# Sparse attention over gathered key blocks, with mixing in full tiles, in a fused attention and mixer kernel

## The chip, the cores and the metric

The kernel runs on one core of one Trainium2 chip. The metric is the device time of one execution in microseconds (us); the figure given is the median of several executions. A profile is one further execution, recorded instruction by instruction.

## The reference

The first half is block-sparse attention (the "BigBird" pattern) over 4 batches, 8 heads, 768 positions and 64 elements a head. Positions form 24 blocks of 32. A block of queries sees its own block and the two neighbours, the first and the last block, and three sampled blocks; the first and the last query block see everything. Which blocks are sampled is an input, `sampled_blocks` of 24 x 3 integers, known only when the kernel runs.

```python
scores = scale * np.matmul(q, k.transpose(0, 1, 3, 2))
mask = np.abs(blk_i - blk_j) <= window
mask = mask | (blk_i == 0) | (blk_j == 0) | (blk_i == n_blocks - 1) | (blk_j == n_blocks - 1)
for qb in range(n_blocks):
    for kb in sampled_blocks[qb]:
        mask[qb * block:(qb + 1) * block, kb * block:(kb + 1) * block] = True
scores = np.where(mask, scores, -1000000000.0)
...
return np.matmul(attn, v).astype(np.float32)
```

The second half mixes. With x the attention's output as (batch, 768, 512), and weights of 768x256, 256x768, 512x1536 and 1536x512:

```python
xt = x.transpose(0, 2, 1)
h = np.maximum(xt @ w_tok1, 0.0) @ w_tok2
u = x + h.transpose(0, 2, 1)
h2 = np.maximum(u @ w_ch1, 0.0) @ w_ch2
return (u + h2).astype(np.float32)
```

A batch's token mixing (`w_tok`) needs all 768 rows of x of that batch; its channel mixing (`w_ch`) needs u of the rows that it treats.

## The kernel before

**Attention.** A step is a pair of heads p (four to a batch, 16 in all), a third t of the queries (256) and a third jj of the keys (256). `scores` (matmul L917) fills two banks of PSUM with keys on the partitions and queries along the row; ScalarE takes the exponential of 128x1024 elements (L930). All 768 keys are computed for every query, and the mask is put in afterwards or beforehand: in batch 0 by 24 more rows in the contraction (88 instead of 64), from batch 1 on by `cut` (L948), a product on VectorE of the exponentials with a mask of zeros and ones that GpSimd has spread over 128x6x768 elements (L731). Then comes the product with V, which carries a column of ones, so that column 65 of the result is the sum of the weights: in batch 0 `pv_stream` (L1086, full tiles of 128 rows), later `pv_halves` through the helper `halves`. VectorE divides by the sum (L1040 and L1041, in batch 0 L1099 and L1100) and writes x.

**Transposes of Q and K.** TensorE does them for pairs 0 to 7 (L823 and L858), SP's transposing DMA for pairs 8 to 15 (`crossbar`, L788).

**`halves`** (L365, matmul L375) computes everything after batch 0's attention, up to the last attention product, in pairs of matmuls on 64-row tiles: one pass over the upper and lower rows of the contraction into two banks, then a fence on SP or GpSimd (L361), then a second pass with the banks exchanged. The scores from batch 1 on are also pairs of 64-row tiles, one head each, so that TensorE keeps one shape of tile throughout. Only after the last attention product does mixing run in full 128-row tiles (`tok_full` L1296 and L1318, `ch` L1536 and L1601).

**Mixing.** `tok` and `tok_first` (batch 0, a pair at a time) do token mixing, `turn_by_crossbar` (L1145, SP) or `turn_by_pe` (L1165) and, for batch 0, `turn_first` transpose u, and `ch` does channel mixing in pieces: first layer, ReLU (ScalarE L1128 or VectorE L1130) into the tile `rc`, second layer, addition on VectorE (L1567, L1615), and a store by SP (L1572, L1626).

**What sets the order.** No engine chooses anything on the chip: a `Planner` (L104) runs at build time and writes every engine's order by hand. It keeps a clock with assumed costs, streams of TensorE work with priorities (scores, attention products, transposes, token and channel mixing), a list of operations for VectorE, ScalarE and SP with costs and due times, and the eight banks of PSUM. A table of knobs (`KN`) changes priorities along the way. `P.phase` is 0 up to the last score of batch 0, 1 while attention is left, 2 after that. Loads of Q, K and V (L447) and of weights (L455, L459, L466, L473) are issued by GpSimd.

Of the kernel before, what the change touches and what calls it, by code (L numbers as in the profile page):

```python
# [12 lines left out]
PLAN = False  # L13
BASE = dict(
    tokp=2.5, trp=2.6, toks=-0.5, back=0.5, relayk=0.8, relayv=3.0, fin=0.9, relu=2.2, cut=0.7,
# [11 lines left out]
    6: dict(fin=4.1, cps=3, trp=1.6),  # L27
    7: dict(fin=4.1, cps=3, trp=1.6),
    8: dict(fin=4.1, cps=3, trp=1.6, add=0.3, back=1.1, cut=0.5),
    9: dict(shift=6000.0),  # L30
    10: dict(fin=4.1, cps=3, trp=1.6, add=0.3, back=1.1, cut=0.5, m2=300.0, ev2=0.9, jit=300.0),
    12: dict(fin=4.1, cps=3, trp=1.6, add=0.3, back=1.1, cut=0.5, m2=300.0, ev2=0.9, jit=300.0, tokp=1.7, backp=0.9, cpo=2, m1=0.0),
    13: dict(fin=4.1, cps=3, trp=1.6, add=0.3, back=1.1, cut=0.5, m2=300.0, ev2=0.9, jit=2000.0, tokp=1.7, backp=0.9, cpo=2, m1=0.0, late=3.5, relayk=0.8),
    14: dict(m2=0.0, cch=2, m1=0.0, cut=6.0, ev4=1.2),
    16: dict(add=0.3, late=1.05, cch=2, ev4=2.0, relayk=3.5),
    17: dict(m1=0.0, back=1.1, add=0.95),
    18: dict(m1=0.0, back=1.1, add=0.95, cut=1.1, m2=300.0, cpo=2),
    19: dict(cps2=3, toks=0.4, jit=300.0, relayv=3.0, relayk=3.5),
    20: dict(m1=0.0, back=1.1, add=0.95, cut=1.1, m2=0.0, cpo=2, toks=-0.5, backp=0.45, cpm=1),
    21: dict(m1=0.0, back=1.1, add=0.95, cut=1.1, m2=0.0, cpo=2, toks=-0.5, backp=0.45, cpm=1),  # L40
    22: dict(m1=100.0, back=1.1, add=0.95, cut=6.0, m2=0.0, cpo=2, toks=-0.5, backp=0.45, cpm=1, relayk=0.8),
    23: dict(m1=100.0, back=1.1, add=0.95, cut=6.0, m2=0.0, cpo=2, toks=-0.5, backp=0.45, cpm=1, relayk=0.8, jit=300.0, cps=3),
    24: dict(m1=100.0, back=1.1, add=0.95, cut=6.0, m2=0.0, cpo=2, toks=-0.5, backp=0.45, cpm=1, relayk=0.8, jit=300.0, cps=3),
    25: dict(jit=450.0, cps2=2, relayv=4.6),
    27: dict(jit=450.0, cps2=2, relayv=4.6, cps=2, backp=0.45, cpo=2, relu=0.85),
    28: dict(jit=450.0, cps2=2, relayv=4.6, cps=2, backp=0.45, cpo=2, relu=0.85),
    29: dict(jit=450.0, cps2=2, relayv=4.6, cps=2, backp=0.45, cpo=2, relu=0.85, toks=0.4, relayk=4.5),
    30: dict(jit=450.0, cps2=2, relayv=4.6, cps=2, backp=0.45, cpo=1, relu=0.85, norm=0.6, cpm=2, backt=0.9),
    31: dict(back=1.1, cpm=1, jit=1300.0),
    32: dict(jit=450.0, cps2=2, relayv=4.6, cps=2, backp=0.45, cpo=1, relu=0.85, norm=1.0, cpm=2, backt=0.9, m1=100.0, shift=0.0),  # L50
    33: dict(tokp=0.7, cps=3, ev4=1.2, shift=-6000.0, cch=2),
    34: dict(chs=0.8, m1=100.0, ev2=1.2, cpo=2, backt=0.2),
    35: dict(jit=0.0, cpo=2, chs=1.1),
# [50 lines left out]
class Planner:  # L104
# [12 lines left out]
    def __init__(self, slots, caps):  # L117
        self.now = 0.0
        self.free_at = {"pe": 0.0, "act": 0.0, "dve": 0.0, "sp": 0.0}
# [93 lines left out]
    def step(self):  # L213
# [36 lines left out]
        for eng in ("act", "dve", "sp"):  # L250
# [9 lines left out]
            for o in self.ops:  # L260
# [4 lines left out]
                if eng == "act" and prio > 0 and self.now + cost["act"] > exp_at + KN["grace"]:  # L265
                    continue
# [28 lines left out]
def kernel(  # L295
# [10 lines left out]
    out: bass.AP,  # L306
):
    nc = tc.nc

    B, H, S, D = q.shape  # L310
    assert (B, H, S, D) == (4, 8, 768, 64)
    NC = 6
    DM, DT, DC = 512, 256, 1536
    NP = B * H // 2
    MASKVAL = -30000.0
    NV = 4
    NR = 4
    NET = KN["net"]
# [46 lines left out]
    def halves(n, cost, outs, lhs, rhs, deps, tags, begin, done, prio, ahead=0.0):  # L365
# [25 lines left out]
        for x in range(n):  # L391
            def emit(x=x):
                if x == 0:
                    begin()
# [1353 lines left out]
```

The softmax here doesn't subtract the row's maximum and nothing guards it: scores larger than these inputs give would overflow.

## Time and profile before

| what | value |
|---|---|
| device time, median of 3 runs | 244.84 us (244.62 to 245.03) |
| the profiled execution, span from first to last instruction | 243.4 us |
| mean granted TensorE clock, 1 is full | 0.999 |
| TensorE (PE) busy | 237.0 us, 97% |
| VectorE (DVE) busy | 172.1 us, 71% |
| ScalarE (ACT) busy | 170.0 us, 70% |
| GpSimd (POOL) busy | 49.5 us, 20% |
| instructions | 9647 |

The profiled execution has no device time of its own but its span, 243.4 us; the median of the runs stands 1.4 us above it. In lines of the profile L12 is line 12 of the kernel. "Busy" adds the durations of an engine's instructions where they don't overlap; "PEld" is the loading of weights into TensorE, which runs beside its matmuls; SPq, POOLq are the sequencers of SP and GpSimd, which issue DMAs, and issuing is not counted as busy. A group's line gives line, engine, operation, out<-in, count, then busy us and mean ns of one, then the engine's idle time just before these instructions and what ended most of it. The time of a matmul in such a line is that from its start to its modelled end, and matmuls overlap.

### The profile page before, as it was taken

Reading aid. Unit: us, or ns where it says so; the run is one execution under the profiler, and the core shown is the slowest. Engines: PE = TensorE matmul, PEld = TensorE weight load, DVE = VectorE, ACT = ScalarE, POOL = GpSimd, SP = SyncE. Lnnn points to the kernel's source line nnn. Section 1 sums busy time; section 2 is a strip of 40 time slices with the busy share of each in tenths; the row PEclk is TensorE's granted clock in tenths of the full one; section 3 lists DMA queues with packets and bytes.
Section 4 is the critical chain, followed back from the end, with each engine's and each line's share of the span. In section 5 each row is a group of like instructions: output and inputs, shape, how many; then the busy total and the mean of one; then the engine's idle time right before and its main releaser. Section 6 shows DMA issues by size and latency. Waiting matters only on the chain.

```text
span 243.4 us, 9647 instructions
## 1 busy us (share of the span) xinstructions
PE 237.0 (97%) x4343; PEld 170.9 (70%) x4343; DVE 172.1 (71%) x285; ACT 170.0 (70%) x187; POOL 49.5 (20%) x86
## 2 busy tenths in 40 slices
PE   7999999999999999999999999999999999999994
PEld 3689999767777677867878667677688664565444
DVE  5975987979899889799789788987687535100222
ACT  6889999868797699788778987798658400366000
POOL 8966987357710000000000000000000000000000
PEclk9999999999999999999999999999999999999999
DMA  7999999999993874131207270501030024200132
GB/s 163 166 214 203 209 207 203 206 201 196 201 180 76 132 167 137 38 118 33 40 3 89 46 155 3 154 25 67 3 67 3 5 89 127 112 3 0 43 132 86
DMA packets 39755, 26.17 MB, mean 108 GB/s; under 512 B 21985, under 2 KB 37105, under 8 KB 39713
## 3 DMA queue, kind: packets, MB, share of 16 engines
q0 software_dynamic: 15104, 12.98, 33.9%
q1 hardware_dynamic: 24064, 12.17, 20.4%
q8 instruction: 34, 0.56, 0.9%
q10 hardware_dynamic: 544, 0.39, 0.6%
q14 instruction: 9, 0.07, 0.1%
HBM read 26.74 MB, written 6.29 MB: 136 GB/s over the span
## 4 chain that ended last, share of the span: by engine, by line
PE 89%; DMA 3%; ACT 3%; POOL 2%; DVE 1%; issue 0%; POOLq 0%; DVEq 0%; ACTq 0%
PE banks L375 53%; PE banks L917 14%; PE banks L1601 9%; PE banks L1536 6%; DMA kraw<-in_k_dram 3%; ACT et L930 3%; PE banks L1086 3%; PE banks L858 1%; PE banks L1354 1%; DVE et L948 1%; POOL vraw L447 1%; PE banks L1296 1%; PE banks L1376 1%; PE banks L1318 1%; POOL ktb L517 0%
## 5 line engine op out<-in xcount | busy, mean ns | idle before, releaser
L930 ACT ACTIVATE et<-banks 128x1024 bf16<-128x1024 f32 x144 | 141.6, 1025 | 28.3 <-PE banks L917 24.5
L948 DVE TENSOR_TENSOR et<-et,mask 128x2976 bf16<-128x2976 bf16 x36 | 61.3, 1703 | 8.3 <-ACT et L930 8.2
L917 PE MATMUL banks<-qtb,ktb 64*128 64x256 bf16 (+1 forms) x576 | 63.7, 270 | 0.7 <-ACT et L930 0.2
L375 PE MATMUL banks<-uT,w_ch 64*128 64x512 bf16 (+1 forms) x576 | 60.6, 322 | 0.0
L375 PE MATMUL banks<-w_ch,rc 64*128 64x512 bf16 x384 | 54.3, 376 | 0.0
L375 PEld LDWEIGHTS <-et 64*128 64x128 bf16 x1728 | 39.2, 94 | 9.4 <-POOLq L361 3.0
L917 PEld LDWEIGHTS <-ktb 64*128 64x128 bf16 (+1 forms) x576 | 33.8, 94 | 15.1 <-issue 1.4
L375 PE MATMUL banks<-vaug,et 64*128 64x65 bf16 x1728 | 42.0, 190 | 0.2 <-issue 0.2
L375 PEld LDWEIGHTS <-w_ch 64*128 64x128 bf16 x576 | 28.6, 94 | 8.4 <-SPq L361 0.6
L1128 ACT ACTIVATE rc<-banks 128x512 bf16<-128x512 f32 (+1 forms) x28 | 21.0, 749 | 17.0 <-PE banks L1536 15.0
L1615 DVE TENSOR_TENSOR o<-banks,x 128x512 f32<-128x512 f32 x7 | 4.8, 692 | 28.2 <-PE banks L1601 28.2
L1130 DVE TENSOR_SCALAR rc<-banks 128x1024 bf16<-128x1024 f32 x17 | 20.8, 1221 | 3.4 <-PE banks L375 3.2
L375 PEld LDWEIGHTS <-rc 64*128 64x128 bf16 x384 | 17.3, 94 | 7.9 <-POOLq L361 0.5
L1601 PE MATMUL banks<-w_ch,rc 128*128 128x512 bf16 (+2 forms) x120 | 21.3, 337 | 0.0
L1601 PEld LDWEIGHTS <-rc 128*128 128x128 bf16 x120 | 10.7, 98 | 10.6 <-issue 0.8
L375 PEld LDWEIGHTS <-w_tok 64*128 64x128 bf16 x288 | 14.5, 109 | 3.3 <-POOLq L361 0.6
L1041 DVE TENSOR_TENSOR x<-banks,recip 128x256 bf16<-128x256 f32 x36 | 15.3, 425 | 1.2
L1536 PE MATMUL banks<-uT,w_ch 128*128 128x512 bf16 (+1 forms) x96 | 15.8, 326 | 0.0
L1536 PEld LDWEIGHTS <-w_ch 128*128 128x128 bf16 x96 | 9.4, 98 | 6.4
L1567 DVE TENSOR_TENSOR o<-banks,x 128x1024 f32<-128x1024 f32 x8 | 9.8, 1224 | 5.1 <-PE banks L375 5.0
L1086 PE MATMUL banks<-vaug,et 128*128 128x65 bf16 x288 | 13.1, 193 | 0.0
L1264 DVE TENSOR_TENSOR x<-banks,x 128x512 bf16<-128x512 f32 (+2 forms) x12 | 10.3, 887 | 2.9 <-PE banks L375 2.7
(122 smaller groups left out, 198.0 us busy)
## 6 DMA issues: line engine op xcount, KB each, us to landing
out_dram<-o SPq DMA_DIRECT2D x8, 512.0 KB, 3.6
w_ch<-in_moe_w_ch_dram POOLq DMA_DIRECT2D x8, 384.0 KB, 9.8
vraw<-in_v_dram POOLq DMA_DIRECT2D x10, 192.0 KB, 7.9
out_dram<-o SPq DMA_DIRECT2D x7, 256.0 KB, 2.0
kraw<-in_k_dram POOLq DMA_DIRECT2D x9, 192.0 KB, 9.2
qraw<-in_q_dram POOLq DMA_DIRECT2D x9, 192.0 KB, 8.3
w_tok<-in_moe_w_tok_dram POOLq DMA_DIRECT2D x2, 384.0 KB, 10.0
qf<-in_v_dram POOLq DMA_DIRECT2D x4, 192.0 KB, 7.8
```

What stands on the lines that cost most here:

```text
L375: mms.append(nc.tensor.matmul(out=outs()[o](x), lhsT=lhs(o, x, r), rhs=rhs(o, x, r), start=(back == 0 and x == 0), stop=(back == 1 and x = ...
L917: nc.tensor.matmul(out=ps[:, hd, 256 * i : 256 * i + 256], lhsT=ktb[n][rows, h, 256 * jj + 128 * i : 256 * jj + 128 * i + 128], rhs=qtb[n] ...
L930: nc.scalar.activation(out=ets[p, t][:, jj, :, :, :].rearrange("k i h q -> k h i q"), in_=ps.rearrange("k h (i q) -> k h i q", i=2), func= ...
L948: nc.vector.tensor_tensor(out=et, in0=et, in1=free(mask[:, 2 * lo, 256 * t + EDGE : 256 * t + EDGE + 1], 0, [[S, 2 * n], [0, 2], [1, w]]), ...
L1041: nc.vector.tensor_tensor(out=free(xs[b][:, pb // 2, 2 * t, 128 * (pb % 2) : 128 * (pb % 2) + 128], 0, [[64, 2], [256, 2], [1, 64]],), in0 ...
L1086: nc.tensor.matmul(out=po[:, hd, c, :], lhsT=et[:, jj, i, hd, 128 * c : 128 * c + 128], rhs=va[:, hd, 2 * jj + i, 0:65], start=(jj == 0 an ...
L1128: nc.scalar.activation(out=o(), in_=src(), func=AF.Relu)
L1130: nc.vector.tensor_scalar(out=o(), in0=src(), scalar1=0.0, scalar2=None, op0=ALU.max)
L1264: nc.vector.tensor_tensor(out=u, in0=src, in1=u, op=ALU.add)
L1536: nc.tensor.matmul(out=in_bank(pbox["pm"], [k, 128 * n])[:, x // 4, :], lhsT=w_ch1[:, x % 4, 128 * cc : 128 * cc + 128], rhs=st[b]["uT"][: ...
L1567: nc.vector.tensor_tensor(out=t[:, :, :].rearrange("p c (g e) -> p g c e", g=2), in0=free(banks[:, pbox["pm"][0], :], 0, [[256, 2], [512, ...
L1601: nc.tensor.matmul(out=pbox["pm"][:, 0:n], lhsT=box["rc"][:, cc, 128 * sc : 128 * sc + 128], rhs=w_ch2[:, cc, lo : lo + n], start=(cc == 0 ...
```

## The change

Batch 0's attention stays as it is. For batches 1 to 3:

- Q, K and V are loaded with eight consecutive rows on each of 96 partitions (L414). TensorE transposes Q and K of all three batches (`turn_kq`, L1081, copies out at L1094 and L1099); SP's transposing DMA for pairs 8 to 15 and the mask with its product go. K of a batch lies in `kA`, in which each pair of neighbouring blocks is followed by the first and the last block (`ends`, L1114).
- The work is cut into chunks of four query blocks, six to a batch, in the order 1, 2, 3, 4, 0, 5. A query block meets eight key blocks: four in `kA` (its own pair, the first, the last) and four in `kB` (three sampled ones and the neighbour outside the pair). VectorE copies two sampled blocks into `kB` from addresses in registers (L1039, 132 copies in all), ScalarE or GpSimd the third (L1047), GpSimd the neighbour (L1056). A block that would be counted twice is sent to rows of zeros.
- V of a batch is copied together (L962), stored to a scratch in DRAM (L972), and loaded back as `va` and `vn` (L981 to L986). For each chunk the gathered rows of V come from that scratch into `vb`: for half of the query blocks by SP, four DMAs a block with addresses in registers (L1004, L1006), for the other half by one indirect DMA of GpSimd a block (L1011).
- Scores (`unit`, L1144): per chunk and two pairs of heads 24 matmuls of 64 or 32 query columns into two banks, and one exponential of 128x1024 (L1195). The first and the last query block are computed against all keys (L1165, exponential of 128x768 at L1173). The product with V (`att_pv`, L1240) is in tiles of 32 columns, one query block each, 128 keys deep, with 65 columns of V, and there is one division for a whole chunk of 512 columns (L1250, L1251).
- Token and channel mixing run in full 128-row tiles throughout, 512 columns a matmul in token mixing (L1347, L1366) and 384 in the first layer of channel mixing (L1484, second layer L1511). The helper `halves` and its fences go. TensorE transposes u of batch 1 (L1316), SP's DMA u of batches 2 and 3. Three tiles hold x instead of four, and `rc` is split in two halves. The Planner also plans GpSimd.

The core of the diff:

```diff
-            def cut(eng, lo=group[0], n=len(group)):
-                w = 256 - 2 * EDGE
-                et = free(ets[p, t][:, lo, 0, 0, EDGE : EDGE + 1], 0, [[512, 2 * n], [256, 2], [1, w]])
-                nc.vector.tensor_tensor(
-                    out=et, in0=et,
-                    in1=free(mask[:, 2 * lo, 256 * t + EDGE : 256 * t + EDGE + 1], 0,
-                             [[S, 2 * n], [0, 2], [1, w]]),
-                    op=ALU.mult,
-                )
...
-        yield from halves(12, 30.5, outs, lhs, rhs, deps, [("po", 2)], begin, done, lambda: KN["backp"])
...
+            def get(eng, b=b, j=j, n=n, qs=mine):
+                t = vb[n % NVB]
+                r = int_range(
+                    vtab[:, 4 * j + qs[0] : 4 * j + qs[-1] + 1, :].rearrange("o q s -> o (q s)"),
+                    len(qs) * NS, nc.sync, S)
+                for i, x in enumerate(qs):
+                    nb = 4 * j + x + (-1 if x % 2 == 0 else 1)
+                    nc.sync.dma_start(out=t[96:128, x, :], in_=stage[b][BLK * nb : BLK * nb + BLK, :])
+                    for s in range(NS):
+                        nc.sync.dma_start(
+                            out=t[32 * s : 32 * s + 32, x, :], in_=stage[b][bass.ds(r[NS * i + s], BLK), :])
...
+                    for x in part:
+                        for s in range(2):
+                            nc.vector.tensor_copy(
+                                out=kB[n % NKB][:, x, :, 32 * s : 32 * s + 32],
+                                in_=kA[b][:, :, bass.ds(kregs["dve", s, 4 * j + x], BLK)])
...
+                if x in inner_q[j]:
+                    work.append((128 + 32 * x, 32, lambda hd, x=x: kB[sc % NKB][64 * hd : 64 * hd + 64, x, g, :], 32 * (lo + x)))
...
+            for i, (at, n, lhs, qat) in enumerate(work):
+                for hd in range(2):
+                    nc.tensor.matmul(
+                        out=ps[:, hd, 256 * r + at : 256 * r + at + n], lhsT=lhs(hd),
+                        rhs=qT[b][64 * hd : 64 * hd + 64, g, qat : qat + n],
+                        start=(r == 0 and i == 0), stop=(r == 1 and i == len(work) - 1),
+                    )
...
+                                    elif turn == 0:
+                                        lhs, rhs = et[:, hd, r, 32 * x : 32 * x + 32], va[:, 2 * j + x // 2, col : col + 65]
+                                        last = 1
+                                    elif turn == 1:
+                                        lhs, rhs = et[:, hd, r, 128 + 32 * x : 160 + 32 * x], vb[sc % NVB][:, x, col : col + 65]
+                                        last = 1
...
+                                    nc.tensor.matmul(
+                                        out=banks[32 * x : 32 * x + 32, bank[ph], at : at + 65], lhsT=lhs, rhs=rhs,
+                                        start=(r == 0 and hd == 0 and turn == 0),
+                                        stop=(r == 1 and hd == 1 and turn == last), skip_group_check=True,
+                                    )
```

Each such 32-column tile of `att_pv` has its own 32 partitions of the bank, so four query blocks (x = 0 to 3) take four neighbouring tiles of the array.

## The prediction

> **What bounds the kernel now.** I read the page first (engine shares, the chain that ended last), then the busy time by stage, then first and last starts of two matmul lines, then short stretches of the timeline for the price of one instruction. The page:
>
> ```profile
> span 243.4 us, 9647 instructions
> ...
> PE 237.0 (97%) x4343; PEld 170.9 (70%) x4343; DVE 172.1 (71%) x285; ACT 170.0 (70%) x187; POOL 49.5 (20%) x86
> ...
> PE 89%; DMA 3%; ACT 3%; POOL 2%; DVE 1%; issue 0%; POOLq 0%; DVEq 0%; ACTq 0%
> ...
> L930 ACT ACTIVATE et<-banks 128x1024 bf16<-128x1024 f32 x144 | 141.6, 1025 | 28.3 <-PE banks L917 24.5
> L948 DVE TENSOR_TENSOR et<-et,mask 128x2976 bf16<-128x2976 bf16 x36 | 61.3, 1703 | 8.3 <-ACT et L930 8.2
> ```
>
> PE carries 89% of the last chain. The exponentials (141.6 us on ACT) and the mask products (61.3 us on DVE), which the change cuts, are on engines with 30% idle. By stage:
>
> ```profile
> 0.00:42.40 42.40, 39.98 (x613) 33.53 (x614) 33.03 (x92) 38.04 (x43) 34.26 (x65) 1.00 1.14 195
> 42.40:60.00 17.60, 16.93 (x374) 12.53 (x372) 15.88 (x23) 13.46 (x15) 9.39 (x14) 1.00 1.28 201
> 150.00:200.00 50.00, 49.98 (x1089) 36.38 (x1086) 35.92 (x46) 32.55 (x34) 0.00 (x0) 1.00 0.17 50
> ```
>
> (Columns: window, its length, busy us of PE, PEld, DVE, ACT, POOL, clock, DMA share, GB/s.) Up to 42.4 us, batch 0, ACT is the limit (38.0 of 42.4, from a first exponential at 6.7). After it PE has no gap, so every us there is PE work. The ends of those stages:
>
> ```profile
> L1086 PE MATMUL banks<-vaug,et x288: 190/193/198, 10.5 to 42.4; 128*128 128x65 bf16 x144
> L1601 PE MATMUL banks<-w_ch,rc x120: 219/379/390, 199.4 to 239.9; 128*128 128x512 bf16 x84, 128*128 128x128 bf16 x24, 128*128 128x256 bf16 x12
> ```
>
> Batch 0's attention ends at 42.4 and the last matmul at 240.1; 3.3 us of addition and store follow to 243.4. The median of the runs, 244.84, is 1.4 above this span; I add the 1.4 to every span.
>
> **Prices on PE.** Matmul durations (190 ns for 65 columns) are latency; the price is start to start:
>
> ```profile
> 20.00 0.65 PE L1086 MATMUL banks<-vaug,et 128*128 128x65 bf16 x16
> 20.48 0.60 PE L917 MATMUL banks<-qtb,ktb 88*128 88x256 bf16 x4
> ...
> 155.35 0.53 PE L375 MATMUL banks<-vaug,et 64*128 64x65 bf16 x24
> 155.72 0.59 PE L375 MATMUL banks<-w_ch,rc 64*128 64x512 bf16 x4
> 156.16 0.38 PE L917 MATMUL banks<-qtb,ktb 64*128 64x256 bf16 x4
> ...
> 197.27 1.48 PE L1296 MATMUL banks<-x,w_tok 128*128 128x256 bf16 x12
> 198.68 0.82 PE L375 MATMUL banks<-w_ch,rc 64*128 64x512 bf16 x6
> ```
>
> Full tile, 65 columns: 0.48/16 = 30 ns (29.5 in the mean). Two 64-row tiles with 65 columns: 0.37/12 = 30.8 ns a pair. Four 64x512: 0.44, so 216 to 220 ns a pair; a full 512 tile costs 216 too, so **full tiles in the mixing buy nothing by themselves**. Going from full to 64-row tiles costs extra: twelve at 109 ns are 1.31 us, the next starts after 1.41, so 0.10 us a switch.
>
> **PE after the change, from batch 0's end on.** Before, 194.4 us of such work remains there: scores 214 pairs x 109.2 ns = 23.4, PV 864 pairs x 30.8 = 26.6, transposes 0.4, mixing 144.0. With the 3.3 us that PE lost this makes the 197.7 from 42.4 to 240.1. After, by the new instruction order: mixing 144.4 (384 matmuls of 384 columns at 162.5 ns = 62.4; 312 of the second layer 62.2; token mixing and its transposes 19.8). Attention of three batches:
> - Scores: 864 matmuls, two 64-row tiles at a time, 288 with 64 columns and 576 with 32. The trace has no 32-column pair; bounds are 32/65 of 30.8 and 30.8. I take 30.8, since weight loads stay 128 wide: 432 pairs = 13.3 us.
> - PV: 1344 matmuls of 65 columns on 32-column tiles, four to a row of the array. Not in the trace. Bounds: four in the time of today's pair (7.7 ns each), none together (29.5). I take 8.7, nearest the pair row, whose second member starts 1 to 2 ns after the first: 11.7 us.
> - 288 quarter tiles for the first and last query block, likewise 8.7: 2.5 us. 352 K/Q transposes of 96 columns (batches 2, 3 came by SP's transpose DMA before), two together, 22 ns (21 to 42.5): 7.7 us.
> - 115 changes of tile shape at 0.10 = 11.5 us; before hardly any. This eats most of the gain: 50.4 becomes 35.2 + 11.5 = 46.7.
>
> So 144.4 + 46.7 = **191.1 against 194.4**. At the bounds of the new tiles: 1.9 less, up to 42 more.
>
> A rule speaks against even this. The Trainium skill, "TensorEngine Tiling (Array Packing)", section Restrictions and Gotchas, says that column tiling excludes the fast weight load; "TensorE: Matmul & The Clock Gate", section LDWEIGHTS, puts a load at its column count over 1.2, so 27 ns for 32 columns. If those loads ran one by one, 1344 would be an estimated 36 us where I count 11.7. No run here shows a 32-column load yet.
>
> **The other engines.** ACT: 144 exponentials become 72 of 1025 ns and 12 narrower; some 60 us go, all off the path. DVE: 61.3 us of mask go; 132 register copies of K blocks come. Prices:
>
> ```profile
> 1.32 0.43 SPq L485 DMA_DIRECT2D kf<-in_k_dram  x1
> 12.53 0.74 SPq L685 DMA_DIRECT2D qtb<-qtb  x1
> ...
> 16.69 2.51 POOL L731 COPY mask<-maskb 128x288 bf16<-128x288 bf16 x6
> ...
> 62.12 0.71 POOL L447 DMA_DIRECT2D qtb<-in_k_dram  x1
> ...
> 25.25 0.35 DVE L762 COPY vaug<-vraw 128x768 bf16<-128x768 bf16 x1
> 26.03 0.18 DVE L1099 RECIPROCAL recip<-banks 128x4 f32<-128x4 f32 x1 [0.44 <-PE banks L1086]
> ```
>
> A K copy of 128x128 lies between 0.18 and 0.35; I take 0.27 with its register step: 36 us, half of what the mask took, free while it stays ahead of the scores.
>
> **The new second bound is SP.** The V gather reads a DRAM copy, half of the query blocks by SP: 44 DMAs of 32 rows a batch. Issue rows are 0.43 and 0.74 (0.34 for a store); I take 0.45, as these have few descriptors. A batch: 44 x 0.45 = 19.8; 33 register steps at 0.1 = 3.3; six register loads at 0.6 = 3.6 (0.18 to 2.4, a small instruction and a store's landing); eight DMAs to stage and reload V 3.6; stores 1.0; transposes 2.9. That is 34 us, 103 for three, while PE needs 99 from the first new score to the last token mixing, with three buffers of lead (some 13 us). It fits on average, not at every place: the store waits on DVE and the V reload waits for the last PV of the batch before, and the gathers queue behind both. Walking the last batch block by block, the fourth gather lands 1.7 us late. POOL has 11 indirect gathers a batch (0.7 to 2, I take 1.1), 12 loads at 0.71, two copies of near blocks a chunk at 0.48 and some K copies: about 29 us a batch, mostly in order behind PE's releases; I give it 2 us of PE waiting.
>
> So after batch 0 PE loses the 3.3 of today, plus 2 by SP, plus 2 by POOL: L = 7.3 (3 to 20). In batch 0 the DVE gets some 20 index operations (0.18 at most: 3.6), 48 registers in three loads (3.0; 0.5 to 7), staging of V (1.4) and K/Q copies (2.0), and loses 4.5: net 5.5 on 33 of 42 busy, ahead of normalisations that release PE. P = 2 (0 to 6).
>
> The Trainium skill, "Runtime: NRT & Kernel Launch", section Instruction fetch mechanics, gives about 200 ns a register for such loads. By it the 48 would hold DVE an estimated 9.6 us and the forecast would rise by some 6; the trace has no such load.
>
> Sum: 42.4 + 2 + 191.1 + 7.3 + 3.3 = 246.1 span, **247.5 us**.
>
> **Rivals.**
> - *The gathers stay ahead* (0.34). P = 0 and L = 3.3: 240.1 span, 241.5 us, faster than before. It decides below P + L = 6.6. For it: the sums above fit the window, and the last 80 us are pure mixing without gathers. Against: SP at 103 of 112.
> - *Column tiles run two at a time* (0.13). PV and quarter tiles at 15.4 ns: +10.9, 258.4 us; with unpaired transposes (42.5) +7.9 more, 266. For it: only pairs are in the trace.
> - *SP's register DMAs cost what the 24-row copies cost* (0.11). 0.74 instead of 0.45 is 12.8 us a batch; SP needs 141 against 112, so 29 late instead of 2: about 274 us. For it: that row is the only short-row DMA.
> - That the change would not do what it says is ruled out by the order: no mask product is left, and mixing has 128-row tiles only.
>
> **How the numbers follow.** The forecast case has 0.42 and spans 243 to 252; its low edge gives 0.05 faster and 0.05 within 0.2% (about 0.5 us, what a measurement here can tell from no change). Faster: 0.34 + 0.05 = 0.39; same 0.05; slower 0.56. The range reaches from 238 (gathers ahead, new tiles between 7.7 and 8.7 ns) to 264 (column tiles by twos). About 0.04 lies below and 0.14 above.
>
> **What would show it.** Right: new PV line busy near 12 us, ACT near 90, SP's issues packed between 45 and 145 us, PE idle before PV or scores with DMA or DVE as releaser, and no idle after the last token mixing. Wrong: PV starts 15 ns or more apart (column tiles), batch 0 ending later than 46 us (registers), or an idle sum under 5 us (gathers ahead).

## The result and the profile after

The changed kernel takes **308.79 us** (305.42 to 310.37, 4 runs) against 244.73 us of the kernel before (median of four runs, three of which are those of the table ahead): a ratio of 1.255 (1.247 to 1.263). The ratio leaves out the run of 310.37 us, which counts as slow (more than 1.5% above the fastest). The forecast was 247.5 us with a range up to 264; it missed by 61 us. The profiled execution took 309.59 us, its span is 307.6. The page after:

```profile
span 307.6 us, 10296 instructions
PE 254.4 (83%) x4292; PEld 159.7 (52%) x4292; DVE 120.0 (39%) x333; ACT 141.4 (46%) x197; POOL 100.7 (33%) x181
PEclk9995999685599799977977985959999999999999
PE 56%; DMA 25%; SPq 5%; POOL 4%; issue 4%; DVE 3%; ACT 1%; POOLq 0%; DVEq 0%
```

PE's share of the last chain falls from 89% to 56%, and DMA's rises from 3% to 25%. The clock row, all nines before, has fives to eights up to slice 27. PE is busy for longer, though VectorE and ScalarE have less to do. What PE waited for (us in total, times, longest):

```profile
PE banks L1240 <- DMA va<-stage: 15.7, 2, 8.8
PE banks L1144 <- POOL kb L1056: 12.9, 1, 12.9
PE banks L1484 <- DMA w_ch<-in_moe_w_ch_dram: 3.9, 3, 1.8
PE banks L1240 <- DMA vb<-stage: 3.5, 2, 2.0
PE banks L1081 <- issue: 2.6, 3, 1.4
PE banks L895 <- DVE vblk L885: 2.4, 1, 2.4
```

Three more lines name `issue`, which means that PE waited for nothing that the profile shows; with the one above they come to 7.6 us, and theory F below takes them up.

**The account.** From PE's records and the clock rows of the trace I add three things between its first and last matmul: idle time; half of the busy time that fell into stretches at half clock ("lost"); and the rest, which is work at full clock. Before: 2.1 idle, 0 lost, 237.0 work, last matmul at 240.1. After: 48.5 idle, 20.2 lost (40.5 of the 254.4 busy at half clock), 234.2 work, last matmul at 303.9. So the change took 2.8 us of PE work away, and 46.4 of idling and 20.2 of slow clock came: 63.8 in all. (One or two per cent of the matmul records are missing in some of the traces; a hole counts as idle, so the three terms are good to some 3 us.)

**The prices on PE were right.** The product with V in 32-column tiles (timeline: start, us, line, tile, shape, count):

```profile
84.61 0.21 PE L1240 MATMUL banks<-va,et_mem 128*32 128x65 bf16 x4
84.64 0.21 PE L1240 MATMUL banks<-vb,et_mem 128*32 128x65 bf16 x4
84.67 0.22 PE L1240 MATMUL banks<-va,et_mem 128*32 128x65 bf16 x4
84.70 0.22 PE L1240 MATMUL banks<-vb,et_mem 128*32 128x65 bf16 x4
84.85 0.23 PE L1144 MATMUL banks<-kq 64*128 64x64 bf16 x4
```

Four side by side every 0.03 us: 8 ns each, where the forecast had 8.7; the change of tile shape at 84.85 costs about 0.1. The estimate of 36 us for their weight loads, made in the forecast from the Trainium skill's "TensorEngine Tiling (Array Packing)" (section Restrictions and Gotchas) and "TensorE: Matmul & The Clock Gate" (section LDWEIGHTS), does not hold here: each of the 1344 matmuls has a weight load of its own (104 ns in the mean), and the starts are 8 ns apart all the same.

**The waits.** GpSimd's queue ahead of the first score:

```profile
58.30 0.96 POOL L1011 DMA_INDIRECT vb<-stage,vidx  x1 [1.16 <-DMA w_ch<-in_moe_w_ch_dram]
61.87 0.90 POOL L431 DMA_DIRECT2D w_tok<-in_moe_w_tok_dram  x1 [2.61 <-DMA w_ch<-in_moe_w_ch_dram]
64.81 0.68 POOL L414 DMA_DIRECT2D rawmem<-in_v_dram  x1 [2.04 <-DMA w_ch<-in_moe_w_ch_dram]
68.03 0.64 POOL L414 DMA_DIRECT2D rawmem<-in_v_dram  x1 [2.54 <-DMA w_ch<-in_moe_w_ch_dram]
71.15 1.25 POOL L414 DMA_DIRECT2D rawmem<-in_v_dram  x2 [2.48 <-DMA w_ch<-in_moe_w_ch_dram]
77.88 0.63 POOL L414 DMA_DIRECT2D rawmem<-in_q_dram  x1 [3.56 <-DMA vb<-stage]
78.50 0.74 POOL L1056 COPY kb<-kq 128x256 bf16<-128x256 bf16 x2
```

Each load waits until an earlier transfer of the same queue has landed, though nothing in the data asks for it. The semaphores in the trace say which one: all 93 DMAs that GpSimd issues signal one of eight semaphores (109 to 116) in rotation when they land, and where an issue waits for a landing, it is on the semaphore that its own landing will signal. So it waits for the transfer eight before it; the load at 64.81, for example, for the load of `w_ch` issued at 46.16, which landed at 64.52. These waits are part of the program as it was built (SP's DMAs have eight semaphores of their own); a rule of the queue itself is not shown by them. The copy of the near K block at 78.50, which the first score needs, stands behind them all. And the reload of V, on SP:

```profile
122.69 0.66 SPq L981 DMA_DIRECT2D va<-stage  x1
123.40 1.59 SPq L982 DMA_DIRECT2D va<-stage  x1
125.04 0.46 SPq L983 DMA_DIRECT2D va<-stage  x1
```

It can only be issued when the last product of the batch before is done (122.7); it moves 2,376 KB (792 + 792 + two of 363 and two of 33), and in the chain of waits it lands 13.25 us after 125.04. From 122 to 138 us the DMA engines are busy throughout (share 1.08, 240 GB/s). In all, the two kinds of DMA queue moved 40.8 MB, before 25.2.

**The clock** (busy us by stretch, the last three columns clock, DMA share and GB/s):

```profile
70.35:73.76 3.41, 0.00 (x0) 0.00 (x0) 0.00 (x0) 0.00 (x0) 2.57 (x5) 0.50 1.20 276
73.76:77.17 3.41, 0.00 (x0) 0.00 (x0) 0.00 (x0) 0.00 (x0) 0.56 (x1) 0.50 1.24 247
77.17:80.59 3.42, 1.49 (x46) 1.19 (x47) 0.43 (x4) 0.77 (x1) 2.36 (x7) 0.50 1.24 208
80.59:84.00 3.41, 3.41 (x35) 1.55 (x32) 1.70 (x7) 1.70 (x3) 2.96 (x8) 0.51 1.21 226
84.00:87.41 3.41, 2.83 (x141) 1.96 (x139) 2.26 (x10) 2.98 (x5) 2.19 (x7) 1.00 0.57 143
```

PE resumes at 78.97 and runs at half clock until 84.00. In this trace the clock changes in steps of 3.41 us. Of the stretches at full clock, as long as PE had work left, each with PE busy for 0.62 of it or less was followed by one at half clock, and none with 0.72 or more was. The border is not sharp: in the run e9 below, stretches with 0.53 and 0.60 kept the full clock.

### The profile page after: what moved, and what is told of

It reads as the page before. It is cut to its first block, busy times and chain, and to the rows that moved or that the text cites. A ratio compares the mean times of both kernels' runs of the same rounds, so it can differ in the third digit from the quotient of the medians.

```text
span 307.6 us, 10296 instructions
## 1 busy us (share of the span) xinstructions
PE 254.4 (83%) x4292; PEld 159.7 (52%) x4292; DVE 120.0 (39%) x333; ACT 141.4 (46%) x197; POOL 100.7 (33%) x181
## 3 DMA queue, kind: packets, MB, share of 16 engines
q0 software_dynamic: 15264, 17.94, 33.4%
## 4 chain that ended last, share of the span: by engine, by line
PE 56%; DMA 25%; SPq 5%; POOL 4%; issue 4%; DVE 3%; ACT 1%; POOLq 0%; DVEq 0%
PE banks L1484 19%; PE banks L1511 19%; DMA va<-stage 8%; PE banks L1240 6%; DMA w_ch<-in_moe_w_ch_dram 6%; DMA w_tok<-in_moe_w_tok_dram 5%; PE banks L1144 3%; SPq L1006 3%; PE banks L1081 2%; DMA rawmem<-in_v_dram 2%; DMA vb<-stage 2%; DMA stage<-vst 2%; PE banks L1347 2%; POOL rawmem L406 1%; PE banks L741 1%
## 5 line engine op out<-in xcount | busy, mean ns | idle before, releaser
L1484 PE MATMUL banks<-uT,w_ch 128*128 128x384 bf16 x384 | 75.3, 350 | 3.9 <-DMA w_ch<-in_moe_w_ch_dram 3.9
L1511 PE MATMUL banks<-w_ch,rc 128*128 128x512 bf16 (+2 forms) x312 | 68.2, 370 | 0.0
L1280 ACT ACTIVATE rc<-banks 128x768 bf16<-128x768 f32 x41 | 33.2, 811 | 68.2 <-PE banks L1484 68.2
L1195 ACT ACTIVATE et_mem<-banks 128x1024 bf16<-128x1024 f32 x36 | 35.6, 1024 | 54.9 <-PE banks L1144 51.5
L1484 PEld LDWEIGHTS <-w_ch 128*128 128x128 bf16 x384 | 37.7, 103 | 31.5 <-issue 5.9
L1511 PEld LDWEIGHTS <-rc 128*128 128x128 bf16 x312 | 28.9, 99 | 30.4 <-issue 1.3
L1011 POOL DMA_INDIRECT vb<-stage,vidx x33 | 32.8, 993 | 23.1 <-PE banks L1240 11.7
L1525 DVE TENSOR_TENSOR o<-banks,x 128x1024 f32<-128x1024 f32 x11 | 13.5, 1223 | 68.0 <-PE banks L1511 61.8
L754 ACT ACTIVATE et_mem<-banks 128x1024 bf16<-128x1024 f32 x36 | 34.5, 1028 | 5.4 <-PE banks L741 5.1
L1240 PEld LDWEIGHTS <-et_mem 128*32 128x32 bf16 x1344 | 20.1, 104 | 27.8 <-issue 25.7
L1240 PE MATMUL banks<-va,et_mem 128*32 128x65 bf16 x528 | 20.1, 213 | 16.9 <-DMA va<-stage 15.7
L741 PE MATMUL banks<-dense 88*128 88x256 bf16 x144 | 23.4, 289 | 1.0 <-ACT et_mem L754 0.5
L1240 PE MATMUL banks<-vb,et_mem 128*32 128x65 bf16 x528 | 20.2, 212 | 4.5 <-DMA vb<-stage 3.5
L1250 DVE RECIPROCAL recip<-banks 128x8 f32<-128x8 f32 x18 | 3.7, 207 | 50.0 <-PE banks L1240 49.9
L1144 PE MATMUL banks<-kq,kb 64*128 64x32 bf16 x176 | 5.1, 177 | 13.4 <-POOL kb L1056 12.9
L1081 PE MATMUL banks<-ident,rawmem 96*64 96x96 bf16 x384 | 11.9, 214 | 2.7 <-issue 2.6
L1144 PEld LDWEIGHTS <-kb 64*128 64x128 bf16 x264 | 6.2, 96 | 13.7 <-POOL kb L1056 13.2
L1039 DVE COPY kb<-kq 128x128 bf16 x44 | 6.6, 223 | 16.4 <-PE banks L1144 16.3
L1081 PEld LDWEIGHTS <-rawmem 96*64 96x64 bf16 x384 | 9.7, 114 | 6.0 <-issue 5.6
L1251 DVE TENSOR_TENSOR x<-banks,recip 128x512 bf16<-128x512 f32 x18 | 12.4, 691 | 0.6
```

The lines of the kernel that those rows point to most:

```text
L741: nc.tensor.matmul(out=ps[:, hd, 256 * i : 256 * i + 256], lhsT=ktb[p][0:88, hd, 256 * jj + 128 * i : 256 * jj + 128 * i + 128], rhs=qtb[p ...
L754: nc.scalar.activation(out=ets[p, t][:, jj, :, :, :].rearrange("k i h q -> k h i q"), in_=ps.rearrange("k h (i q) -> k h i q", i=2), func= ...
L1011: nc.gpsimd.indirect_dma_start(out=vb[n % NVB][:, x, :], out_offset=None, in_=stage[b], in_offset=bass.IndirectOffsetOnAxis(ap=vidx[:, 4 * ...
L1081: nc.tensor.matmul(out=t[64 * hd : 64 * hd + 64, c, :], lhsT=raws[nm, p][:, hd, c, :], rhs=ident[0:96, 0:96], start=(c == 0), stop=(c == 7 ...
L1144: nc.tensor.matmul(out=ps[:, hd, 256 * r + at : 256 * r + at + n], lhsT=lhs(hd), rhs=qT[b][64 * hd : 64 * hd + 64, g, qat : qat + n], star ...
L1195: nc.scalar.activation(out=ets_of[n % 6][:, :, :, :].rearrange("k h r s -> k h (r s)"), in_=ps, func=AF.Exp, scale=0.125)
```

## The experiments

Theory A: the loss is these waits and the half clock behind each, one by one. Theory B, the rival from the forecast: SP's 132 gather DMAs, 99 of them with register addresses, are the limit. Theory C: the clock falls from the kind of work or from DMA load, not from idleness. D and F came later. All runs are compared with the kernel before on the same chip, 245.2 us. The account of each, in us:

| run | time | idle | lost to half clock | work |
|---|---|---|---|---|
| changed kernel | 308.8 | 48.5 | 20.2 | 234.2 |
| e1_v_once | 289.7 | 37.4 | 16.6 | 231.8 |
| e2_no_sp_gather | 296.4 | 44.6 | 16.0 | 230.6 |
| e3_k_copies_off_pool | 302.8 | 50.1 | 14.6 | 231.7 |
| e4_filled_waits | 310.6 | 31.5 | 11.4 | 260.2 (26 of them fillers) |
| e5_order_by_measured_delays | 300.7 | 39.7 | 15.7 | 237.9 |
| e6_order_and_queues | 291.3 | 33.4 | 13.5 | 237.7 |
| e7_reload_in_pieces | 278.1 | 25.1 | 12.4 | 235.1 |
| e9_no_v_transfers | 272.8 | 25.7 | 6.6 | 234.6 |
| e10_small_tiles_spaced (profile of a run of 284.2) | 281.8 | 32.5 | 12.0 | 233.5 |
| e11_spaced_no_v_transfers | 266.1 | 20.6 | 8.7 | 231.6 |
| f1_full_tiles_alone | 272.5 | 2.3 | 0 | 263.0 |

### One cause at a time

**e1_v_once**

```diff
         def whole(eng):
+            if b > 1:
+                return
```

> This kernel leaves out part of the work: V is loaded back from the DRAM scratch (L981 to L986) for batch 1 alone, and batches 2 and 3 use batch 1's. Every engine's order is otherwise that of the changed kernel. Theory A (a few waits of TensorE for transfers, each followed by stretches at half clock): the two waits for this reload, 6.95 and 8.77 us, go, and with them the half clock that follows (some 4 us): 309 becomes about 289 (283 to 296). Theory B (SP's 132 gather DMAs with register addresses are the limit): the gathers are all still there, so no more than 3 us go.

Measured 289.68 us: 19.1 less, as theory A said. The wait for `va` is gone from PE's list.

**e2_no_sp_gather**

```diff
             def get(eng, b=b, j=j, n=n, qs=mine):
+                if n >= NVB:
+                    return
```

> This kernel leaves out part of the work: SP gathers V and loads registers for the first three chunks alone, 15 later chunks use what is in the buffers. Every other queue's order is that of the changed kernel. Theory A: only the waits for gathered V go (3.5 us) and about 5 us at half clock behind them; the 7 us waits for the reload may get shorter since SP comes to it sooner: about 300 (293 to 306). Theory B: SP is the limit, so 25 us or more go: below 284.

Measured 296.38 us: 12.4 less, inside A's range. B falls as the limit, but SP was no bystander: one of the two waits for the reload is gone as well. That reload is issued at 163.18 instead of 174.90; that it no longer stands behind gathers is the likely reason, not shown by itself. In the changed kernel SP's own prices were below those of the forecast (least/median/most ns):

```profile
L1006 SPq DMA_DIRECT2D vb<-stage x99: 315/316/1807, 46.2 to 211.1; - x99
L843 SPq TENSOR_LOAD <-vtab x18: 667/725/2448, 40.9 to 206.8; - x18
L843 DVEq TENSOR_LOAD <-ktab x3: 1108/1119/1339, 22.7 to 25.3; - x3
```

0.32 where 0.45 was taken, and 0.73 where 0.6 was; VectorE's 48 registers took 3.6 us in three loads (3.0 forecast), not the 9.6 estimated in the forecast from the Trainium skill's 200 ns a register ("Runtime: NRT & Kernel Launch", section Instruction fetch mechanics).

**e3_k_copies_off_pool**

```diff
             def get2(eng, b=b, j=j, n=n, qs=qs):
+                eng = "act" if ("act", 2, 0) in kregs else eng
...
-                    nc.gpsimd.tensor_copy(
+                    nc.vector.tensor_copy(
                         out=free(k0, 0, [[512 * 2, len(xs_)], [128, 4], [1, 32]]),
```

> The copies of the near K block (L1056) go from GpSimd to VectorE and those of the third sampled block (L1047) to ScalarE, in the same places of the order; GpSimd keeps the loads and the indirect gathers. Theory A: the first score no longer waits behind loads that GpSimd cannot issue yet, so the wait of 12.9 us shrinks to a few us (the first reload of V and the indirect gathers may come late next), and the half clock from 70 to 84 us goes: about 296 (291 to 303). Theory B: no change beyond 3 us.

Measured 302.76 us: 6.0 less, at the slow end of A's range. The wait of 12.9 us for GpSimd is gone (the first scores run from 61.98 to 62.7), but PE then waited 17.7 us in three pieces for `va` (15.7 in two before): the first reload, a wait of 4.6, had been hidden behind the K copy and came late next. Another 5.1 us went to an exponential that stood on ScalarE behind a copy of V, whose load ScalarE awaited for 10.4 us.

**e4_filled_waits**

```diff
     def unit(b, j, ph, ps, sc):
         lo = 4 * j
+        if sc == 0 and ph == 0:
+            warm(ps[:, 0, :], 56)
...
                 bank = P.bank("po", 2, rel)
+                if j == ORDER[0] and b > 1:
+                    warm(banks[:, bank[0], :], (0, 0, 29, 37)[b])
```

> In front of the three long waits of TensorE (12.9, 6.95, 8.77 us) stand 56, 29 and 37 matmuls of 512 columns on constants (216 ns each, 12.1, 6.3 and 8.0 us), which write a bank that the next work overwrites. They add no wait and remove none. Theory A with the clock following TensorE's own idleness: the waits stay, but the work behind them runs at full clock, 7 us less: about 302 (299 to 305), and the half-clock stretches at 70 to 84, 135 to 142 and 183 to 193 us vanish. Theory C (the clock falls from the kind of work or from the DMA load, not from idleness): the stretches stay and the time is 309 or more.

Measured 310.63 us: nothing gained, against the expectation of 302. The time is in theory C's range, but the clock is not as C has it: the half clock behind the three waits did go (lost 20.2 to 11.4, mean clock 0.900 to 0.955), so it does follow PE's idleness and C falls. The time so won was waited away again (idle and fillers 57.5 against 48.5): the third wait ends at 188.30 in both traces (below, first the changed kernel, then e4), and the last attention matmul at 215.4 and 215.6:

```profile
188.30 0.25 PE L1240 MATMUL banks<-va,et_mem 128*32 128x65 bf16 x4 [8.77 <-DMA va<-stage]
188.30 0.21 PE L1251 MATMUL banks<-va,et_mem 128*32 128x65 bf16 x4 [1.19 <-DMA va<-stage]
```

Up to there PE's speed does not set the pace; the transfers do. This is where theory A as a sum fails.

### The clock by itself, where PE sets the pace

Both in the kernel before, in the last stage of mixing; `pause` puts a small matmul, copies on GpSimd and a matmul that needs them ahead of a group:

```diff
+        nc.tensor.matmul(out=o, lhsT=zt[:, 0, 0:128], rhs=zt[:, 0, 0:128], start=True, stop=True)
+        for _ in range(13):
+            nc.gpsimd.tensor_copy(out=zt[:, 0, :], in_=zt[:, 1, :])
+        nc.tensor.matmul(out=o, lhsT=zt[:, 0, 0:128], rhs=zt[:, 0, 0:128], start=True, stop=True)
```

> The kernel before, with one pause in its last stage of channel mixing, where TensorE has no gap otherwise: a small matmul, 13 copies of 128x288 on GpSimd (0.42 us each by the rows of the mask copies), a small matmul that needs the last copy. About 5.7 us of idle. If the clock follows idleness (the changed kernel's profile: stretches of 3.4 us that hold less than two thirds of work are followed by stretches at half clock), the time grows by the pause and by one or two stretches at half clock, 1.7 to 3.4 us: 244.8 + 5.7 + 2.6 = about 253. If not, by the pause alone: 250.5.

> The same, with six pauses of one such copy each, 4 us or more apart (about 0.9 us of idle each, 5.4 in all, a quarter of a 3.4 us stretch). If it is the idle share of a stretch that counts, no stretch falls to half clock and the time is 244.8 + 5.4 = 250.2; if any idleness lowers the clock, 255 or more.

Measured 254.50 us for one pause (6.47 idle) and 250.49 us for six (0.62 idle each). Busy time and clock by stretch, first one pause, then six:

```profile
211.44:214.86 3.42, 2.39 (x16) 1.36 (x14) 0.00 (x0) 2.16 (x4) 0.83 (x2) 1.00 0.09 33
214.86:218.27 3.41, 0.00 (x0) 0.00 (x0) 0.00 (x0) 0.00 (x0) 2.98 (x8) 1.00 0.00 0
218.27:221.68 3.41, 1.38 (x8) 1.01 (x9) 0.00 (x0) 0.00 (x0) 1.73 (x5) 0.51 0.02 5
221.68:225.10 3.42, 3.42 (x11) 1.38 (x10) 0.00 (x0) 1.19 (x2) 0.00 (x0) 0.50 0.00 0
```

```profile
211.48:214.89 3.41, 2.79 (x23) 2.01 (x22) 0.00 (x0) 1.79 (x3) 0.42 (x1) 1.00 0.00 0
218.30:221.72 3.42, 2.79 (x23) 2.03 (x22) 0.00 (x0) 1.79 (x3) 0.43 (x1) 1.00 0.00 0
```

The empty stretch is followed by two at half clock, which cost 2.4 us on top of the 6.5. Stretches that stay busy for 2.79 of 3.41 us keep the full clock. So half clock costs in full where PE is the limit; in the changed kernel the 8.8 us of it that e4 took away had cost nothing, because a transfer was late anyway. The Trainium skill ("TensorE: Matmul & The Clock Gate", section HAM oscillation — how this bites in real kernels) warns of idle gaps over about 3.4 us; in the changed kernel the drop came with stretches that still held 0.62 of work.

### Order and queues, with nothing left out

Theory D: the waits are filled if mixing, of which 88 us (215.4 to 303.9) were left at the end, is put into them. The order is written from assumed delays, so the Planner is told the measured ones.

**e5_order_by_measured_delays**

```diff
-            ("sp",), {"sp": 2800.0}, [stored, va_read[b - 1] if b > 1 else pv_done[NT0 - 1]], whole, prio=1, lat=4500.0))
+            ("sp",), {"sp": 2800.0}, [stored, va_read[b - 1] if b > 1 else pv_done[NT0 - 1]], whole, prio=1, lat=13000.0))
...
-    RATE = 200.0
+    RATE = 130.0
```

> The changed kernel's instructions in another order: the Planner is told the measured delays (V reload 13 us instead of 4.5, a gathered block 2.2 us of SP instead of 1.6, loads at 130 instead of 200 bytes a ns with eight in flight, store of V 5 us), nothing else. Theory D (after the filled waits brought nothing): up to 205 us the pace is set by transfers, and 99 us of mixing are left at the end because the order puts waiting attention work ahead of mixing that is ready; told the delays, mixing fills the waits: 270 (260 to 285), with less than 25 us idle. Theory A as it stood (the waits add up in any order): 300 or more.

Measured 300.69 us, a miss for theory D: 8 less instead of 39, which is the number that theory A had. The two waits for `va` are gone from PE's list, but those for `w_ch` grew to 6.8 and many of 0.3 to 2 us came in their place, and work rose by 3.7. Changes of tile shape are not the reason (108 after batch 0's attention, 116 in the changed kernel); it stays open.

**e6_order_and_queues**

```diff
                 if not got or min(got)[0] > P.now + 500.0:
-                    return
+                    early = [y for y in loads if y in (load_ch1, load_ch2)]
+                    if not early or x[0] == "v":
+                        return
+                    loads.remove(early[0])
+                    loads.appendleft(early[0])
+                    continue
```

> As the one before, and the near and third K copies on VectorE and ScalarE, and the loads of the channel weights issued as soon as GpSimd would wait for a free buffer of K and Q. Theory D: TensorE gets channel mixing of batch 0 some 15 us earlier, and the first scores no longer wait behind loads: 258 (250 to 270). Theory A: 290 or more.

On top of e5, it lets the loads of the channel weights pass a load of K or Q that waits for a free buffer, and moves the K copies as in e3. Measured 291.34 us: 9.4 less than e5, a miss for theory D (250 to 270) and inside A's "290 or more". No wait for `w_ch` is left.

**e7_reload_in_pieces**, on top of e6:

> As e6_order_and_queues, with the reload of V for batches 2 and 3 cut into six pieces of three DMAs, each issued as soon as that chunk's product of the batch before is done, and the part for the first and last query block on its own. Nothing is left out. If the burst of the reload is what holds up the attention of the next batch: 283 (276 to 288). If it is SP's issue time (18 DMAs a batch instead of 5, some 4 us more), it gets slower: 294 to 300.

```diff
-            ("sp",), {"sp": 2800.0}, [stored, va_read[b - 1] if b > 1 else pv_done[NT0 - 1]], whole, prio=1, lat=13000.0))
...
+        for j in ORDER:
...
+            alias(va_set[b, j], P.op(("sp",), {"sp": 1700.0}, [stored, pv_read[b - 1, j]], piece, prio=1, lat=4500.0))
```

Measured 278.10 us: 13.2 less than e6, within the range for the burst of the reload as the cause; SP's issue time would have made it slower. This is the fastest version that computes everything, still 1.132 (1.126 to 1.137) times the kernel before.

### What is left

**e9_no_v_transfers**: e6 without the reloads that e1 leaves out, the gathers that e2 leaves out, and GpSimd's gathers.

```diff
         def whole(eng):
+            if b > 1:
+                return
...
             def get(eng, b=b, j=j, n=n, qs=mine):
+                if n >= NVB:
+                    return
...
             def get2(eng, b=b, j=j, n=n, qs=theirs):
+                if n >= NVB:
+                    return
```

> This kernel has the order of e6_order_and_queues and leaves out part of the work: after the third chunk, V is neither gathered (SP and GpSimd) nor loaded back for batches 2 and 3. K copies, scores, products and mixing are all there. If V's transfers cause what is still lost against the kernel before (46 us): 258 (250 to 265). If the K path, ScalarE and the supply of instructions to TensorE cause it: 275 or more.

Measured 272.79 us: between the two expectations. Of the 46.1 us that e6 loses against the kernel before, V's transfers are 18.5, the smaller part, and 27.6 remain. In its timeline:

```profile
98.49 0.19 PE L1245 MATMUL banks<-vb,et_mem 128*32 128x65 bf16 x1
101.71 0.24 PE L1245 MATMUL banks<-vb,et_mem 128*32 128x65 bf16 x3 [3.03 <-issue]
```

PE stops for 3.03 us inside a row of four matmuls and waits for nothing that the profile shows. Counted from the first, the ten stops of this kind, 12.5 us in all, fall on PE's instruction numbers 194 modulo 256 (2242, 2498, 2754, 3010 and so on), and in the changed kernel nine of them, 7.5 us, on 193 to 195. The instruction queue on the changed kernel's page has 33 packets, 0.54 MB in all, 16 KB each; PE's 8642 instructions, its waits included, are 33 times 256 and a rest. Theory F: one such packet brings 256 instructions, and matmuls of 8 ns use those up (a weight load and a matmul each, so 128 matmuls) in 1.05 us and outrun the supply. The Trainium skill ("Runtime: NRT & Kernel Launch", section Instruction fetch mechanics) also says that instructions come in blocks of 16 KiB, 256 of them; that the fetch is hidden, as it says too, does not hold for the burst of the next run. To measure it in the kernel before, 720 additional matmuls like L1240's, in one burst or in 15 of 48:

```diff
+        for i in range(720):
+            x = 32 * (i % 4)
+            nc.tensor.matmul(out=o[x : x + 32, 0:65], lhsT=mask[:, 0, x : x + 32], rhs=mask[:, 1, 0:65],
+                             start=True, stop=True, skip_group_check=True)
```

> The kernel before with 720 additional matmuls of 65 columns on 32-column tiles (four side by side) in one burst in the last stage, on data that is there; their result is overwritten. If their price is 8.2 ns whatever stands beside them: 5.9 us and 0.2 us for two changes of tile shape, 245 + 6.1 = 251.2. If TensorE outruns its supply of instructions (theory F: 256 instructions are 128 such matmuls, 1.05 us, and the next 256 take longer to come): stops of 0.5 to 1.5 us after every 256 instructions, five or six of them, and stretches at half clock: 256 to 262.

> The same 720 matmuls in 15 bursts of 48 (0.4 us each), 1.5 us or more apart among the mixing matmuls. 5.9 us and 30 changes of tile shape at 0.10: 245 + 8.9 = 254, by either theory; with theory F no stop at multiples of 256, so it is faster than the one burst in spite of 28 more changes of shape.

Measured 264.95 us in one burst, above the range of theory F, because the stops are longer than expected, and 254.59 us spread, as forecast. The burst:

```profile
214.14 1.95 PE L371 MATMUL banks<-mask 128*32 128x65 bf16 x128 [2.37 <-issue]
217.87 1.95 PE L371 MATMUL banks<-mask 128*32 128x65 bf16 x128 [1.78 <-issue]
221.32 1.95 PE L371 MATMUL banks<-mask 128*32 128x65 bf16 x128 [1.50 <-issue]
224.77 1.95 PE L371 MATMUL banks<-mask 128*32 128x65 bf16 x128 [1.51 <-issue]
228.23 0.93 PE L371 MATMUL banks<-mask 128*32 128x65 bf16 x53 [1.50 <-issue]
```

Exactly 128 matmuls, a stop, 128 matmuls, a stop: five stops, 8.7 us, and the half clock that they bring (5.4 lost). The DMA engines have little else to do (share 0.05 from 210 to 232 us). Spread out, each burst takes its 0.4 us and none stops:

```profile
213.01 0.56 PE L371 MATMUL banks<-mask 128*32 128x65 bf16 x48
213.50 1.92 PE L1553 MATMUL banks<-uT,w_ch 128*128 128x256 bf16 x16
```

So F is shown for such a burst, and the DMA records of the traces show it for the other kernels too: every one of these stops ends 1.2 to 1.6 us after a packet of PE's instruction queue has come in, all nine in the changed kernel (before 99.71 the packet of 97.46 to 98.42), all six in e7 and all ten in e9. In the burst a packet starts 1.1 us after PE has resumed, takes about 1.0, and PE resumes another 1.3 to 1.4 us later: 256 instructions every 3.45 us (3.73 the first time). In e9 the packet for the resumption at 101.71 started only 3.06 us after the resumption before it, with a DMA share of 1.00 in that stretch; that the load on the DMA engines delays it is likely, not shown.

Two runs tried to take the stops out by spacing (e10 is e7, e11 is e9, both with the Planner made to put 1.5 us of full tiles behind every 88 or so small matmuls):

```diff
+                        if mode == 0:
+                            self.debt = max(0.0, self.debt - cost)
+                        elif self.phase:
+                            self.tiny += {1: 24, 2: 64, 3: 32, 4: 24}.get(mode, 3)
+                            if self.tiny >= 88:
+                                self.tiny, self.debt = 0, 1500.0
```

> As e7_reload_in_pieces, and the Planner puts 1.5 us of full-tile mixing (where any is ready) behind every 88 matmuls on small tiles, and places the three matmuls of the index table 5 us later. Theory F: the stops of 1 to 3 us at multiples of 256 instructions between 92 and 125 us go, and with them the half clock there: 278 becomes 264 (256 to 270). If the stops are waits for other engines: 274 or more.

> As e9_no_v_transfers (after the third chunk V is neither gathered nor loaded back: part of the work is left out), with small tiles spaced and the index table's matmuls later as in e10_small_tiles_spaced. Theory F: 273 becomes 256 (250 to 262). If the stops are waits for other engines: 268 or more.

Measured 281.79 us and 266.07 us: the first on the side of the rival (274 or more), the second between the two (262 to 268). With V's transfers left out, spacing brings 6.7 of the 17 us that were expected; with them it brings nothing (e7 had 278.1). The stops became fewer but did not go: six of 11.5 us in all in e7 became three of 5.3 in e10, and ten of 12.5 in e9 became six of 7.8 in e11, one of them 4.10 long. In e10 the spaced order ran into other waits, and the index table's matmuls, placed later, waited longer for VectorE (4.4 us). What e11 still has over the kernel before is 18.5 of idle and 8.7 at half clock, less some 5 of work: 9 of the idle lie before 57 us, in batch 0 and its index table, 8 between 92 and 109 us, of which 7.3 are four of these stops. The rest was not taken apart further.

### Full tiles alone

```diff
-        if P.phase == 1:
+        if False:
```

> The kernel before with one half of the change alone: token and channel mixing in full 128-row tiles throughout, attention as before on 64-row tiles (u of batch 1 is transposed by SP's DMA instead of TensorE). By the rows of before a full 512-column matmul costs what a pair on 64 rows costs (216 and 218 ns), so mixing gains nothing, and each change of tile shape costs 0.10 us; some 60 to 120 of them: 252 (247 to 258). If full tiles do bring something: below 244.

Measured 272.46 us: 27.3 slower with attention untouched, a miss by 15 us beyond its upper end. No wait and no half clock; it is all work (263.0 against 237.0), in the timeline:

```profile
103.71 0.39 PE L1601 MATMUL banks<-w_ch,rc 128*128 128x512 bf16 x1
104.03 0.36 PE L375 MATMUL banks<-vaug,et 64*128 64x65 bf16 x12
104.22 0.38 PE L917 MATMUL banks<-qtb,ktb 64*128 64x256 bf16 x4
104.44 0.35 PE L375 MATMUL banks<-vaug,et 64*128 64x65 bf16 x12
104.72 0.39 PE L1601 MATMUL banks<-w_ch,rc 128*128 128x512 bf16 x1
```

From 103.71 to 104.03 are 0.32 us for one 512-column matmul of 0.216: a change of shape is 0.10, as priced. There are some 270 of them in the trace, not 60 to 120 (in the kernel before 20), because attention and mixing alternate in pieces of a matmul or two. That is what the helper `halves` had been saving.

## Why the prediction was wrong

- **PE's work** (191.1 against 194.4, so 3.3 less): right, as far as the account can tell (2.8 less, good to some 3 us). The products with V at 8 ns stand, and so do 115 changes of shape (116 in the trace) at 0.10. Small errors in it offset each other: the trace has 384 transposes of K and Q, not 352 (0.7 us more at the forecast's 22 ns; its +7.9 us for unpaired ones goes by 384, with 352 it is 7.2), and the score pairs of 32 columns start 25 ns apart, not 30.8 (four of them between 84.92 and 85.02). Its "1.9 less" leaves out the lower bound of these pairs, 15.2 ns, worth another 4.5 us. The 3.3 us "that PE lost" before are what its prices left over; the trace has 0.7 us of idle time after 42.4. The forecast's ceiling of gain was sound; it was the only thing to be gained.
- **L = 7.3, PE's loss after batch 0**: the step that failed. Its SP part counted the time to issue ("eight DMAs to stage and reload V 3.6") and no time to land. The reload's landing, 11 to 13 us, comes after the last product of one batch and before the first of the next, with one buffer; the text named that order ("the V reload waits for the last PV of the batch before") and priced it at nothing. PE waited 15.7 us for it; without it the kernel is 19.1 us faster.
- **GpSimd "2 us of PE waiting"**: 12.9 in one piece. The loads were priced by their 0.71 us of issue, not by the wait for earlier loads to land, which the trace of before also has (eight semaphores in rotation; its loads waited up to 1.4 us each, with no copy behind them that PE needed at once).
- **The clock**: no term at all. It was 1.00 in each stage before, because PE had no gap. 20.2 us of the account stand there; e4 shows that 8.8 of them lay under transfers that were late anyway, p1 that half clock costs in full otherwise.
- **Mixing as cover**: "the last 80 us are pure mixing without gathers" was put forward as room. It was the reverse: mixing that is left for the end is cover that the waits did not get. The order is fixed at build by assumed delays (4.5 us for a reload of 13).
- **P = 2 for batch 0**: 4.3 (last product with V starts at 46.7 instead of 42.4). PE waits 2.4 us for the index chain on VectorE, and the clock is halved for 6.8 us behind it, from 22.5 to 29.4. The forecast's sign for slow register loads, batch 0 ending later than 46, came all the same, though the registers took 3.6 against 3.0.
- **Instructions**: 8 ns a matmul was taken as the whole price; g1 shows that a row of more than 128 of them cannot keep it. By g1's 256 instructions every 3.45 us, such a matmul with its weight load would cost an estimated 27 ns in a long row. In the changed kernel 7.5 us of idle time are such stops.
- **ACT near 90**: 141.4 busy. By the forecast's own rows (170.0 less some 60) it would have been 110, and ScalarE took 41 of the 48 ReLUs and many copies. In the changed kernel this cost nothing that could be seen (PE waited 1.7 us for ScalarE).
- **The rivals**: column tiles by twos, wrong (8 ns). SP's DMAs at 0.74, wrong (0.32), though taking them out gains 12.4 through the queue they stand in. "Gathers keep ahead", wrong.

Two terms were thus mis-sized, one was missing, and they fed each other. What stays open is the split of the last 21 us (e11), and how much of e7's remaining 33 would go with a better order.

## What to carry to other kernels

Where one engine is busy 97% of the time without a gap, look first at what a change can take from that engine (here 2.8 us), and then price each new transfer from issue to landing at the place where its buffer comes free; queue occupancy is not enough. In a queue that runs in order, put nothing that the critical engine needs at once behind loads that may have to wait for earlier loads. Where a load waits, look at which semaphore it waits on: here the wait was for the transfer eight before it, and the order of issue decides which one that is. Small tiles have three more prices: the change of shape, the supply of instructions, and the clock when they leave gaps. Bursts of 48 among long matmuls did not stop (g2), but f1 shows what many changes of shape cost.

## What the runs showed of the hardware

- Half clock follows idleness in steps of 3.41 us: in p1 an empty stretch was followed by two at half clock (2.4 us lost); in p6 stretches busy for 0.82 cost nothing.
- A burst of 32-column matmuls stops after every 128 for 1.5 to 2.4 us, with a DMA share of 0.05; the stops end 1.3 to 1.4 us after a 16 KB packet of instructions (g1).
- In these programs the issue of a DMA waits until the one eight before it on its queue has landed, up to 3.6 us at a time on GpSimd; the trace shows the semaphores that do this, not a rule of the queue.
- Four 32-column tiles run side by side at 8 ns a matmul, each with a weight load of its own.
